# Half-height score products of two head pairs in one visit instead of two, from batch 3 on

## The chip, the cores and the metric

The kernel runs on one core of one Trainium2 chip. The metric is the device time of one execution in microseconds; of several runs the median is given. Before the change it is 300.1 us, the median of three runs (300.06 to 301.02). All durations below come from one profiled execution of that kernel.

## The reference

Two stages in a row. First, attention over 8 batches, 8 heads, 576 positions and 64 channels a head. Heads 0 to 3 see the last 32 positions ("local"), heads 4 to 7 see all earlier positions that are equal modulo 32 ("strided"):

```python
mask_local = (rel >= 0) & (rel < stride)
mask_strided = (rel >= 0) & (pos[None, :] % stride == pos[:, None] % stride)
attn = softmax(where(mask, scale * q @ k.T, -1e9)) @ v      # cut
x = attn_out.transpose(0, 2, 1, 3).reshape(4608, 512)
h = x @ w_in                                  # 512 -> 2048
g = np.maximum(h, 0.0) + alpha * np.minimum(h, 0.0)
return g @ w_out                              # 2048 -> 512
```

Second, the two-layer network on the 4608 tokens that come out. Inputs and output are float32.

## The kernel before

**The network.** The 4608 tokens are taken as nine chunks of 512 (the loop over n from L1019). A chunk has 30 steps. Steps 0 to 15 are *lin1* (`lin1_piece`, L688): one block of 128 hidden units, four products 128x512 (L678) into one of three PSUM banks `hb`, which `hbank` lends in turn; ScalarE makes `neg` (L697), VectorE makes `gT` from `neg` and the bank (L700). Steps 16 to 29 are *lin2* (`lin2_sums`, L775): eight products 128x256 a step (L811), seven block products in place of eight, by a Strassen-like scheme that works on sums of quadrants of `gT` (`gsum`, L760). VectorE makes most of these sums at the start of lin2; three slices of the first one, for k-blocks 0 to 5, are made by GpSimd in lin1 steps 5, 9 and 13. The three `hb` banks serve lin2 as accumulators A, B and C.

**Attention.** Heads go in pairs; pair g is pair g mod 4 of batch g // 4, pairs 0 and 1 of a batch local, 2 and 3 strided. A local pair has six blocks of 96 queries against 128 keys, a strided pair eight blocks of 72 against 72 (positions are sorted by their rest). The two heads of a pair lie in partitions 0 to 63 and 64 to 127, so that a score product uses one half of TensorE's rows, and the products of the two heads alternate: these are the half-height products (L450). `score_both` (L427) computes a pair's scores in two groups: the first into the double bank `sp`, the second into two banks of the three-bank pool `ps` (`sph`). ScalarE takes the exponential into a tile `et` (L464, L474), GpSimd multiplies by the mask (L468, L470, L477). The last exps are kept in the list `defer` and let go one by one by `attn_step` (L653), or at once where a PV piece needs them. `pv_piece` (L486) multiplies masked scores with v (L512, two or three pieces of up to six products a pair, each into a `ps` bank); VectorE divides by the row sum (L521, L523). `x_piece` (L530) transposes the result on TensorE (`xp`, a `ps` bank as well), or a DMA does (`x_dma`).

**The order.** A list of pieces is written out in L577 to L645: the step for g holds the scores of pair g, then the PV pieces of pair g - 1, with transposes, loads and copies between them. In the loop from L1019 a counter takes pieces from this list between the steps of a chunk: about one after each lin2 step, one after every two lin1 steps. `keep` (`keep_in_program_order`) holds every engine to the order in which the program was written, so an instruction that waits holds up what stands behind it on its engine. Scores of local pairs fall into lin2, those of strided pairs into lin1.

Of the kernel before, what the change touches and what calls it, by code (L numbers as in the profile page):

```python
# [9 lines left out]
F32 = mybir.dt.float32  # L10
F16 = mybir.dt.float16
ALU = mybir.AluOpType
AF = mybir.ActivationFunctionType
# [19 lines left out]
def kernel(  # L33
# [42 lines left out]
    mfirst, mother, mstr = mmul[:, 0:288], mmul[:, 96:192], mmul[0:72, 288:360]  # L76
# [22 lines left out]
    kTs = [cpool.tile([128, 2, (768, 672)[i]], F16, name=f"kT{i}") for i in range(2)]  # L99
    vls = [cpool.tile([128, 24, 65], F16, name=f"vl{i}") for i in range(2)]  # L100
    vss = [cpool.tile([128, 4, 8, 65], F16, name=f"vs{i}") for i in range(2)]
    ets = [cpool.tile([128, 800], F16, name=f"et{i}") for i in range(NE)]
    x16s = cpool.tile([80, 1024], F16)
    qks = {nm: cpool.tile([80, 4, 512], F16, name=f"{nm}sd") for nm in "qk"}

# [4 lines left out]
    def load_qk(b, strided, nm):  # L110

        h0 = 4 if strided else 0
        src = q if nm == "q" else k
        if strided and b:
            t16 = hpool.tile([128, 2, 512], F16, tag=f"{nm}s", bufs=2, name=f"{nm}s")
            cast16[(b, True, nm)] = t16
        else:
            t16 = hpool.tile([128, 2, 512], F32, tag=f"{nm}l", bufs=2, name=f"{nm}l")  # L120
            loaded[(b, strided, nm)] = t16
        base = src[b, h0 : h0 + 1, 0:1, :]
        eng = nc.sync if (b > 2 and not strided) or (b == 0 and strided) else nc.gpsimd
        if b == 0 and strided and nm == "q":
            eng = nc.scalar
        keep(eng.dma_start(t16, bass.AP(
            tensor=base.tensor, offset=base.offset,
            ap=[[8 * D, 64], [2 * S * D, 2], [S * D, 2], [1, 8 * D]])))
# [30 lines left out]
            keep(nc.sync.dma_start_transpose(o, qks[nm].rearrange("p h c -> p (h c)")))  # L159

    def cast_s(b, nm, eng):
        t16 = hpool.tile([128, 2, 512], F16, tag=f"{nm}s", bufs=2, name=f"{nm}s")
# [77 lines left out]
    def make_pair(g):  # L240
        P = Pair()
        P.g, P.b, P.hp = g, g // 4, g % 4
        P.strided = P.hp >= 2
        P.pr = P.hp % 2
        P.n, P.w = (8, 72) if P.strided else (6, 96)
        u = g // 2
        P.dx = P.b >= DX and P.strided
        P.lx = P.b >= LX and not P.strided
        P.xd = P.b >= DX and P.hp < (2 if P.b == DX else 3)
        if P.dx or P.lx:  # L250
            P.qT, P.kT = (z[u % 2].rearrange("r e c -> r (e c)") for z in (qTs, kTs))
# [4 lines left out]
        if P.lx:  # L256
            P.sgroups = ([0, 1, 2, 3], [4, 5])
        P.et = {}
        P.x16 = None
        return P  # L260
# [162 lines left out]
    defer, defer_et = [], {}  # L423
    late = []
    second = {"on": False}

    def score_both(P):  # L427

        w, r = P.w, 72 if P.strided else 128
        for i in range(2):  # L430
            et = ets[ectr["i"] % NE]
            ectr["i"] += 1
            if i:
                sps = [pspool.tile([128, 512], F32, tag="ps", name="sph") for _ in range(2)]
            else:
                sp = pbpool.tile([128, 2, 512], F32, tag="sp", name="sp")
                sps = [sp[:, y] for y in range(2)]
            grp = P.sgroups[i]
            n = w * len(grp)
            for x, t in enumerate(grp):  # L440
                if P.dx:
                    q0 = k0 = 80 * (4 * (2 * P.pr + t % 2) + t // 2)
                elif P.lx:
                    j = 3 * (2 * P.pr + t % 2) + t // 2
                    q0, k0 = 96 * j, 128 * j
                else:
                    q0, k0 = w * t, 32 + 72 * t if P.strided else 96 * t
                for y in range(2):
                    hf = slice(64 * y, 64 * y + 64)
                    keep(nc.tensor.matmul(  # L450
                        sps[y][:, w * x : w * x + w], P.kT[hf, k0 : k0 + 128],
                        P.qT[hf, q0 : q0 + w], start=(x == 0), stop=(x == len(grp) - 1),
                        skip_group_check=True))
                    P.et[(2 * (t // 2) + y, t % 2) if P.dx or P.lx else (t, y)] = (et, n * y + w * x)
            ev = et[0:r, 0 : 2 * n]
            if not P.strided and i == 0 and not P.lx:
                mv = ev.rearrange("r (y c) -> r y c", y=2)
                m = mfirst.unsqueeze(1).to_broadcast([r, 2, n])
            else:
                z = 2 * w if P.lx and i == 0 else 0  # L460
                mv = ev[:, z:].rearrange("r (c f) -> r c f", f=w)
                m = (mstr if P.strided else mother).unsqueeze(1).to_broadcast([r, (2 * n - z) // w, w])
            if i == 0:
                keep(nc.scalar.activation(  # L464
                    ev.rearrange("r (y c) -> r y c", y=2), sp[0:r, :, 0:n], AF.Exp, scale=SCALE))
                if P.lx:
                    fv = ev[:, 0 : 2 * w].rearrange("r (c f) -> r c f", f=w)
                    keep(nc.gpsimd.tensor_tensor(  # L468
                        fv, fv, mfirst[:, 0:96].unsqueeze(1).to_broadcast([r, 2, w]), op=ALU.mult))
                keep(nc.gpsimd.tensor_tensor(mv, mv, m, op=ALU.mult))  # L470
                continue

            def ex(y):
                keep(nc.scalar.activation(  # L474
                    ev[:, n * y : n * y + n], sps[y][0:r, 0:n], AF.Exp, scale=SCALE))
                if y:
                    keep(nc.gpsimd.tensor_tensor(mv, mv, m, op=ALU.mult))  # L477

            defer_et["et"] = et
            if second["on"]:  # L480
                ex(0)
                defer.append(lambda: ex(1))
            else:
                defer.extend([lambda: ex(0), lambda: ex(1)])

    def pv_piece(P, a):  # L486
        run_masks(P)
        while defer and any(P.et[z][0] is defer_et["et"] for z in P.et):
            defer.pop(0)()
        if P.x16 is None:  # L490
            if P.xd and P.strided:
                P.x16 = x16s
# [25 lines left out]
        w = P.w  # L518
# [52 lines left out]
    def Pv(g, i):  # L571
        return lambda: pv_piece(pairs[g], i)
# [4 lines left out]
    for g in range(7, npair + 2):  # L577
        c = g // 4
# [3 lines left out]
        okT = 8 <= t < 4 * LX and (t % 4 == 0 or t < 4 * DX and t % 2 == 0)  # L582
        nP = len(pairs[p].pgroups) if okP else 0
        seq = []
        if okA:
            seq.append(("S", lambda a=a: score_both(pairs[a])))
        if okP:
            seq.append(("P", Pv(p, 0)))
# [7 lines left out]
            seq.append(("Tk", T(t // 2, "k")))  # L596
        if nP == 3:
            seq.append(("P", Pv(p, 2)))
        if not seq:
            seq.append(("N", lambda: None))  # L600

# [51 lines left out]
    def attn_step(end):  # L653
        run_masks()
        if pos["i"] < end:
            pieces[pos["i"]][1]()
            pos["i"] += 1
        while late:
            late.pop(0)()
        if defer:  # L660
            defer.pop(0)()


    gTs = {}
# [94 lines left out]
        }[which]  # L759
        keep(eng.tensor_tensor(o[:, k0:k1], x[:, k0:k1], y[:, k0:k1], op=op))  # L760

    lay, held = {}, {}

    def store(n, i, j, osb, mts=(0, 1)):

# [310 lines left out]
```

## Time and profile before

| what | value |
|---|---|
| median of three runs | 300.1 us (300.06 to 301.02) |
| the profiled execution | 300.0 us, its span 298.1 us |
| VectorE, ScalarE, GpSimd busy | 76%, 58%, 57% of the span |
| the chain that ended last | PE 80%, DMA 11%, POOL 4%, issue 2%, DVE 2%, ACT 1% |
| a lin1 product 128x512, a lin2 product 128x256 | 379 ns, 272 to 273 ns from start to modelled end |
| exp of 576 columns, of 768 | 654 ns (128 partitions), 811 ns |
| a mask of 576, of 384 columns on GpSimd | 1.27 us, 0.91 us |
| a sum of 512, 1024, 2048 columns on VectorE | 538, 683, 1213 ns |
| a slice of the first sum on GpSimd | 1.15 us |

How to read it: PE is TensorE, PEld its weight loads, which run beside the products; DVE is VectorE, ACT ScalarE, POOL GpSimd, SP the queue of SyncE. A line "out<-in" names the tiles; L and a number is the line of the kernel. Ends of products are modelled, starts are recorded, so two products are compared from start to start. In brackets a view shows how long an engine was idle before an instruction, and what released it. The chain is followed back from the last instruction, at each step to what released it.

### The profile page before, as it was taken

The numbers are of one execution on the slowest core, as the hardware profiler recorded it, in microseconds if no ns is written. First come the engines' busy times: TensorE is split into PE (matmuls) and PEld (weight loads), VectorE is DVE, ScalarE is ACT, GpSimd is POOL, SyncE is SP. The second block draws the span as 40 slices with busy tenths as digits, with TensorE's granted clock in tenths as the row PEclk, the third lists the DMA queues.
The fourth block names the chain that finished last, engine by engine and source line by source line (L and its number), as shares of the span: only waits on it lengthen the run. The fifth ranks groups of instructions, "written<-read, shape, count | busy, mean of one in ns | idle before, by whom it ended". The sixth has DMA issues, their size and how long they took to land.

```text
span 298.1 us, 7107 instructions
## 1 busy us (share of the span) xinstructions
PE 289.9 (97%) x2808; PEld 193.6 (65%) x2808; DVE 227.8 (76%) x427; ACT 173.5 (58%) x325; POOL 168.5 (57%) x182
## 2 busy tenths in 40 slices
PE   7899998999999999999999999999999999999995
PEld 3664445644886478646898887468746864784584
DVE  5788868979975988488848894889488858946872
ACT  3566556888557773776377636763676257406620
POOL 8952289359757996777777778665555003101300
PEclk9999999999999999999999999999999999999999
DMA  7999999995998969999999999993811140022004
GB/s 219 204 202 207 205 238 266 170 175 178 177 154 186 111 100 127 173 192 160 132 209 177 138 141 182 184 144 54 201 22 21 24 141 0 2 71 73 0 2 141
DMA packets 102273, 41.01 MB, mean 138 GB/s; under 512 B 80720, under 2 KB 99424, under 8 KB 102240
## 3 DMA queue, kind: packets, MB, share of 16 engines
q0 software_dynamic: 56336, 19.25, 61.1%
q1 hardware_dynamic: 45632, 20.78, 35.3%
q10 hardware_dynamic: 272, 0.52, 0.6%
q8 instruction: 22, 0.36, 0.6%
q14 instruction: 11, 0.09, 0.1%
HBM read 38.60 MB, written 9.44 MB: 161 GB/s over the span
## 4 chain that ended last, share of the span: by engine, by line
PE 80%; DMA 11%; POOL 4%; issue 2%; DVE 2%; ACT 1%; POOLq 0%
PE hb L678 36%; PE hb L811 32%; DMA ks<-in_k_dram 6%; PE pv L512 4%; DMA win<-in_moe_w_in_dram 3%; PE sp L450 2%; DMA ql<-in_q_dram 2%; PE hb L715 2%; PE opl L811 1%; PE xp L533 1%; PE tp L280 1%; DVE gT L700 1%; PE sph L450 1%; POOL ql L217 1%; POOL vl L205 0%
## 5 line engine op out<-in xcount | busy, mean ns | idle before, releaser
L678 PE MATMUL hb<-xT,win 128*128 128x512 f16 (+1 forms) x616 | 127.2, 357 | 0.0
L700 DVE SCALAR_TENSOR_TENSOR gT<-neg,oma,hb 128x512 f16<-128x512 f32 x138 | 100.7, 744 | 33.0 <-ACT neg L697 26.3
L697 ACT ACTIVATE neg<-hb 128x512 f32<-128x512 f32 x138 | 82.1, 597 | 32.7 <-PE hb L678 31.5
L678 PEld LDWEIGHTS <-win 128*128 128x128 f16 x640 | 60.0, 98 | 53.8
L760 POOL TENSOR_TENSOR gsum<-gT 128x512 f16<-128x512 f16 x23 | 26.5, 1152 | 68.9 <-DVE gT L700 68.9
L811 PEld LDWEIGHTS <-gsum 128*128 128x128 f16 x512 | 47.3, 98 | 6.0 <-DVE gsum L760 0.5
L811 PEld LDWEIGHTS <-gT 128*128 128x128 f16 x384 | 35.9, 98 | 6.0 <-issue 0.5
L470 POOL TENSOR_TENSOR et<-et,mmul 128x576 f16<-128x576 f16 (+1 forms) x24 | 30.6, 1274 | 14.6 <-issue 7.8
L823 ACT COPY o<-hb 128x512 f32<-128x512 f32 (+1 forms) x32 | 18.1, 569 | 32.5 <-PE hb L811 32.5
L523 DVE TENSOR_TENSOR x<-pv,rc 96x384 f16<-96x384 f32 (+2 forms) x65 | 34.5, 531 | 2.2
L811 PE MATMUL hb<-wout,gT 128*128 128x256 f16 x248 | 30.8, 273 | 0.1
L811 PE MATMUL hb<-wout,gsum 128*128 128x256 f16 x248 | 30.5, 272 | 0.0
L811 PE MATMUL hb<-wsum,gsum 128*128 128x256 f16 x248 | 30.3, 273 | 0.0
L477 POOL TENSOR_TENSOR et<-et,mmul 72x576 f16<-72x576 f16 (+2 forms) x24 | 29.3, 1220 | 0.4 <-ACT et L474 0.4
L826 DVE TENSOR_TENSOR o<-hb,o 128x512 f32<-128x512 f32 (+1 forms) x24 | 16.3, 681 | 17.0 <-PE hb L811 12.5
L464 ACT ACTIVATE et<-sp 72x576 f16<-72x576 f32 (+2 forms) x24 | 16.4, 685 | 20.6 <-PE sph L450 17.2
L512 PEld LDWEIGHTS <-et 72*128 72x128 f16 (+1 forms) x416 | 21.9, 98 | 8.0 <-issue 1.3
L474 ACT ACTIVATE et<-sph 72x288 f16<-72x288 f32 (+2 forms) x48 | 17.8, 388 | 0.0
L521 DVE RECIPROCAL rc<-pv 72x6 f32<-72x6 f32 (+2 forms) x80 | 14.5, 181 | 2.9 <-PE pv L512 2.4
L715 PE MATMUL hb<-wout,gT 128*128 128x512 f16 x64 | 15.6, 379 | 0.2 <-ACT osb L720 0.2
L811 PE MATMUL hb<-wsum,gT 128*128 128x256 f16 x120 | 15.3, 273 | 0.0
L760 DVE TENSOR_TENSOR gsum<-gT 128x512 f16<-128x512 f16 (+2 forms) x17 | 14.7, 865 | 0.2
(117 smaller groups left out, 318.0 us busy)
## 6 DMA issues: line engine op xcount, KB each, us to landing
out_dram<-o SPq DMA_DIRECT2D x31, 256.0 KB, 3.1
stv<-in_v_dram POOLq DMA_DIRECT2D x8, 288.0 KB, 8.4
vl<-in_v_dram POOLq DMA_DIRECT2D x6, 384.0 KB, 9.3
wout<-in_moe_w_out_dram POOLq DMA_DIRECT2D x4, 512.0 KB, 16.9
qsd<-in_q_dram POOLq DMA_DIRECT2D x6, 288.0 KB, 7.6
ksd<-in_k_dram POOLq DMA_DIRECT2D x6, 288.0 KB, 7.1
kl<-in_k_dram SPq DMA_DIRECT2D x3, 512.0 KB, 5.1
ql<-in_q_dram POOLq DMA_DIRECT2D x3, 512.0 KB, 6.4
```

The lines of the kernel that those rows point to most:

```text
L470: keep(nc.gpsimd.tensor_tensor(mv, mv, m, op=ALU.mult))
L474: keep(nc.scalar.activation(ev[:, n * y : n * y + n], sps[y][0:r, 0:n], AF.Exp, scale=SCALE))
L477: keep(nc.gpsimd.tensor_tensor(mv, mv, m, op=ALU.mult))
L512: keep(nc.tensor.matmul(pv[:, 65 * x : 65 * x + 65], et[0:r, c : c + 128], v16[0:r, 2 * P.pr + hh, t, :] if P.strided else v16[:, 6 * (2 * ...
L523: keep(nc.vector.tensor_tensor(P.x16[0:w, c0 : c0 + 64 * nb].rearrange("r (c e) -> r c e", e=64), pvv[:, :, 0:64], rc[0:w, 0:nb].unsqueeze ...
L678: keep(nc.tensor.matmul(hps[:, dst : dst + w], win16[:, kk, 128 * m : 128 * m + 128], xT[:, kk, src : src + w], start=(first and kk == kks ...
L697: keep(nc.scalar.activation(neg, hps, AF.Relu, scale=-1.0))
L700: keep(nc.vector.scalar_tensor_tensor(gTs[n][:, m, :], neg, oma[:, m : m + 1], hps, op0=ALU.mult, op1=ALU.add))
L715: keep(nc.tensor.matmul(ops, gTs[n][:, kf, 128 * mt : 128 * mt + 128], wout16[:, kf, :], start=(kf == 0), stop=(kf == 15)))
L760: keep(eng.tensor_tensor(o[:, k0:k1], x[:, k0:k1], y[:, k0:k1], op=op))
L811: keep(nc.tensor.matmul(dst, lhs[:, kf, 128 * mt : 128 * mt + 128], rhs[:, kf, :], start=(first and own and kf == 0), stop=(kf == 7), skip ...
L823: keep(nc.scalar.copy(o, x))
```

## The change

From batch 3 on (`units`), the scores of both pairs of a unit (two local or two strided pairs of a batch) are computed in one visit, `score_unit`. It stands at the end of the step of the unit's first pair, behind the PV pieces of the pair before, with an empty piece ("N") ahead of it and one behind. The step of the unit's second pair has no scores. Batch 2 keeps `score_both`.

A visit uses six banks: `sp` (two) for all but the last block of the first pair A, three `ps` banks, and one lin1 bank or, in lin2, accumulator C before its use. c3 and c4 take the last block of both pairs, for one head each, c1 and c2 the other blocks of pair B. Exps go into new tiles: e1 for A, e2 for B (two sets of each, 1088 wide), e3 for the last blocks. The order on ScalarE is c4, e1, then c3, c1, c2, of which the last three (in lin2 the last two) go through `defer`, now a list of tiles and functions. Masks are two operations for e1, one for e3, two for e2.

```diff
-    ets = [cpool.tile([128, 800], F16, name=f"et{i}") for i in range(NE)]
+    ets = [cpool.tile([128, 640], F16, name=f"et{i}") for i in range(NE)]
+    evs = [[cpool.tile([128, 1088], F16, name=f"ev{i}{j}") for j in range(2)] for i in range(2)]
...
-            t16 = hpool.tile([128, 2, 512], F16, tag=f"{nm}s", bufs=2, name=f"{nm}s")
+            t16 = evs[b]["qk".index(nm)][:, 0:1024].rearrange("p (f c) -> p f c", f=2)
...
+    def score_unit(u):
+        A, Bp = pairs[2 * u], pairs[2 * u + 1]
+        w, r, nb = A.w, 72 if A.strided else 128, 7 if A.strided else 5
+        n = nb * w
+        (e1, e2), e3 = evs[u % 2], ets[u % 2]
+        sp = pbpool.tile([128, 2, 512], F32, tag="sp", name="sp")
+        c3, c1, c2 = [pspool.tile([128, 512], F32, tag="ps", name="sph") for _ in range(3)]
+        c4 = lay["Cf"] if second["on"] else hbank()
+        rest = [(A, nb), (Bp, nb)]
+        streams = [
+            [(A, s, sp[:, 0], w * s) for s in range(nb)]
+            + [(P, s, c3, w * z) for z, (P, s) in enumerate(rest)]
+            + [(Bp, s, c1, w * s) for s in range(nb)],
+            [(A, s, sp[:, 1], w * s) for s in range(nb)]
+            + [(P, s, c4, w * z) for z, (P, s) in enumerate(rest)]
+            + [(Bp, s, c2, w * s) for s in range(nb)],
+        ]
+        for x in range(2 * nb + 2):
+            for y in range(2):
+                P, s, o, c = streams[y][x]
...
+                hf = slice(64 * y, 64 * y + 64)
+                keep(nc.tensor.matmul(
+                    o[:, c : c + w], P.kT[hf, k0 : k0 + 128], P.qT[hf, q0 : q0 + w],
+                    start=(c == 0), stop=(c == (1 if s == nb else nb - 1) * w), skip_group_check=True))
...
+        def masks(e):
+            ev = e[0:r, 0 : 2 * n]
+            if A.lx:
+                fv = ev[:, 0 : 2 * w].rearrange("r (c f) -> r c f", f=w)
+                mask(fv, mfirst[:, 0:96].unsqueeze(1).to_broadcast([r, 2, w]))
+                fv = ev[:, 2 * w :].rearrange("r (c f) -> r c f", f=w)
+                mask(fv, mother.unsqueeze(1).to_broadcast([r, 2 * nb - 2, w]))
+                return
+            k = 4 if A.strided else 3
...
+        ex(e3[0:r, 2 * w : 4 * w], c4[0:r, 0 : 2 * w])
+        ex(e1[0:r, 0 : 2 * n].rearrange("r (y c) -> r y c", y=2), sp[0:r, :, 0:n])
+        masks(e1)
+        if second["on"]:
+            ex3()
+        else:
+            defer.append(((e3,), ex3))
+        defer.append(((e2,), lambda: ex(e2[0:r, 0:n], c1[0:r, 0:n])))
+        defer.append(((e2,), ex2))
...
-        while defer and any(P.et[z][0] is defer_et["et"] for z in P.et):
-            defer.pop(0)()
+        used = [P.et[t, y][0] for t in P.pgroups[a] for y in range(2)]
+        while any(e is z for es, _ in defer for e in es for z in used):
+            defer.pop(0)[1]()
...
-        if okA:
+        units = g >= 4 * (DX + 1)
+        visit = okA and units and a % 2 == 0
+        if okA and not units:
             seq.append(("S", lambda a=a: score_both(pairs[a])))
...
+        if visit:
+            seq.append(("N", lambda: None))
+            seq.append(("S", lambda a=a: score_unit(a // 2)))
+            seq.append(("N", lambda: None))
...
-            for t in ets:
-                keep(nc.gpsimd.memset(t[:, 640:800], 0.0))
+            for t in evs[0] + evs[1]:
+                keep(nc.gpsimd.memset(t[:, 1024:1088], 0.0))
```

The tiles `evs` also serve, in batches 0 and 1, as the staging tiles of the strided q and k. The branches of `score_both` for the transposed local layout (`P.lx`, batches 5 to 7) go, since those batches are now units.

More of the change, by code (lines that the diff above doesn't have):

```diff
@@ L161, in cast_s @@
     def cast_s(b, nm, eng):
-        t16 = hpool.tile([128, 2, 512], F16, tag=f"{nm}s", bufs=2, name=f"{nm}s")
+        t16 = evs[b]["qk".index(nm)][:, 0:1024].rearrange("p (f c) -> p f c", f=2)
         if eng[0] == eng[1]:
@@ L255, in make_pair @@
         P.pgroups = ([0, 1, 2], [3, 4, 5], [6, 7]) if P.strided else P.sgroups
-        if P.lx:
-            P.sgroups = ([0, 1, 2, 3], [4, 5])
         P.et = {}
@@ L421, in score_piece, with mask, ex, ex3 @@
         keep(nc.gpsimd.tensor_tensor(ev, ev, m, op=ALU.mult))
-    defer, defer_et = [], {}
+    defer = []
     late = []
+    lay = {}
     second = {"on": False}
+    def score_unit(u):
[18 more added lines that the diff above has]
+                P, s, o, c = streams[y][x]
+                if P.dx:
+                    q0 = k0 = 80 * (4 * (2 * P.pr + s % 2) + s // 2)
+                elif P.lx:
+                    j = 3 * (2 * P.pr + s % 2) + s // 2
+                    q0, k0 = 96 * j, 128 * j
+                else:
+                    q0, k0 = w * s, 96 * s
+                hf = slice(64 * y, 64 * y + 64)
+                keep(nc.tensor.matmul(
+                    o[:, c : c + w], P.kT[hf, k0 : k0 + 128], P.qT[hf, q0 : q0 + w],
+                    start=(c == 0), stop=(c == (1 if s == nb else nb - 1) * w), skip_group_check=True))
+                key = (2 * (s // 2) + y, s % 2) if P.dx or P.lx else (s, y)
+                P.et[key] = (e3, 2 * w * y + c) if s == nb else (e1 if P is A else e2, n * y + c)
+        def mask(v, m):
+            keep(nc.gpsimd.tensor_tensor(v, v, m, op=ALU.mult))
+        def masks(e):
[7 more added lines that the diff above has]
+            k = 4 if A.strided else 3
+            fv = ev.rearrange("r (y c) -> r y c", y=2)
+            if A.strided:
+                m = mstr
+                for lo, hi in ((0, k), (k, nb)):
+                    mask(fv[:, :, w * lo : w * hi].rearrange("r y (c f) -> r y c f", f=w),
+                         m.unsqueeze(1).unsqueeze(1).to_broadcast([r, 2, hi - lo, w]))
+            else:
+                mask(fv[:, :, 0 : w * k], mfirst.unsqueeze(1).to_broadcast([r, 2, w * k]))
+                mask(fv[:, :, w * k :].rearrange("r y (c f) -> r y c f", f=w),
+                     mother.unsqueeze(1).unsqueeze(1).to_broadcast([r, 2, nb - k, w]))
+        def ex(o, i):
+            keep(nc.scalar.activation(o, i, AF.Exp, scale=SCALE))
+        def ex3():
+            ev = e3[0:r, 0 : 4 * w]
+            ex(ev[:, 0 : 2 * w], c3[0:r, 0 : 2 * w])
+            mask(ev.rearrange("r (c f) -> r c f", f=w),
+                 (mstr if A.strided else mother).unsqueeze(1).to_broadcast([r, 4, w]))
+        def ex2():
+            ex(e2[0:r, n : 2 * n], c2[0:r, 0:n])
+            masks(e2)
+        ex(e3[0:r, 2 * w : 4 * w], c4[0:r, 0 : 2 * w])
[3 more added lines that the diff above has]
+            ex3()
+        else:
+            defer.append(((e3,), ex3))
+        defer.append(((e2,), lambda: ex(e2[0:r, 0:n], c1[0:r, 0:n])))
+        defer.append(((e2,), ex2))
@@ L442, in score_both @@
                     q0 = k0 = 80 * (4 * (2 * P.pr + t % 2) + t // 2)
-                elif P.lx:
-                    j = 3 * (2 * P.pr + t % 2) + t // 2
-                    q0, k0 = 96 * j, 128 * j
                 else:
@@ L453, in score_both @@
                         skip_group_check=True))
-                    P.et[(2 * (t // 2) + y, t % 2) if P.dx or P.lx else (t, y)] = (et, n * y + w * x)
+                    P.et[(2 * (t // 2) + y, t % 2) if P.dx else (t, y)] = (et, n * y + w * x)
             ev = et[0:r, 0 : 2 * n]
-            if not P.strided and i == 0 and not P.lx:
+            if not P.strided and i == 0:
                 mv = ev.rearrange("r (y c) -> r y c", y=2)
@@ L459, in score_both @@
             else:
-                z = 2 * w if P.lx and i == 0 else 0
-                mv = ev[:, z:].rearrange("r (c f) -> r c f", f=w)
-                m = (mstr if P.strided else mother).unsqueeze(1).to_broadcast([r, (2 * n - z) // w, w])
+                mv = ev.rearrange("r (c f) -> r c f", f=w)
+                m = (mstr if P.strided else mother).unsqueeze(1).to_broadcast([r, 2 * n // w, w])
             if i == 0:
@@ L465, in score_both @@
                     ev.rearrange("r (y c) -> r y c", y=2), sp[0:r, :, 0:n], AF.Exp, scale=SCALE))
[L466 to L469, printed above, removed]
                 keep(nc.gpsimd.tensor_tensor(mv, mv, m, op=ALU.mult))
@@ L477, in ex @@
                     keep(nc.gpsimd.tensor_tensor(mv, mv, m, op=ALU.mult))
-            defer_et["et"] = et
             if second["on"]:
                 ex(0)
-                defer.append(lambda: ex(1))
             else:
-                defer.extend([lambda: ex(0), lambda: ex(1)])
+                defer.append(((et,), lambda: ex(0)))
+            defer.append(((et,), lambda: ex(1)))
     def pv_piece(P, a):
         run_masks(P)
-        while defer and any(P.et[z][0] is defer_et["et"] for z in P.et):
-            defer.pop(0)()
+        used = [P.et[t, y][0] for t in P.pgroups[a] for y in range(2)]
+        while any(e is z for es, _ in defer for e in es for z in used):
+            defer.pop(0)[1]()
         if P.x16 is None:
@@ L660, in attn_step @@
         if defer:
-            defer.pop(0)()
+            defer.pop(0)[1]()
     gTs = {}
@@ L760, in g_sum @@
         keep(eng.tensor_tensor(o[:, k0:k1], x[:, k0:k1], y[:, k0:k1], op=op))
-    lay, held = {}, {}
+    held = {}
     def store(n, i, j, osb, mts=(0, 1)):
```

## The prediction

> **What bounds the kernel now.** I read four views in this order. The page first, for the busy engine and its clock:
>
> ```profile
> PE 289.9 (97%) x2808; PEld 193.6 (65%) x2808; DVE 227.8 (76%) x427; ACT 173.5 (58%) x325; POOL 168.5 (57%) x182
> ...
> PEclk9999999999999999999999999999999999999999
> ```
>
> TensorE is busy for 97% of 298.1 us, at full clock in every slice. Whatever makes it issue later lengthens the run; work elsewhere counts only when TensorE waits for it. Next the timeline of PE alone (start, duration, group), in the lin1 half and in the lin2 half of a chunk:
>
> ```profile
> 125.41 0.35 PE L512 MATMUL pv<-vl,et 128*128 128x65 f16 x6
> 125.59 2.75 PE L678 MATMUL hb<-xT,win 128*128 128x512 f16 x12
> 128.28 0.30 PE L450 MATMUL sp<-qT,kT 64*128 64x72 f16 x8
> 128.41 0.29 PE L450 MATMUL sph<-qT,kT 64*128 64x72 f16 x8
> 128.64 2.76 PE L678 MATMUL hb<-xT,win 128*128 128x512 f16 x12
> ...
> 141.26 1.91 PE L811 MATMUL hb<-wsum,gsum 128*128 128x256 f16 x16
> 143.10 0.34 PE L450 MATMUL sp<-qT,kT 64*128 64x96 f16 x8
> 143.28 0.25 PE L450 MATMUL sph<-qT,kT 64*128 64x96 f16 x4
> 143.47 1.05 PE L811 MATMUL hb<-wsum,gsum 128*128 128x256 f16 x8
> 144.59 0.34 PE L512 MATMUL pv<-vs,et 72*128 72x65 f16 x6
> ```
>
> Ends are modelled, so I count from start to start. Spacings: 0.216 us for a 512-wide L678 product (8 from 131.43 to 133.15), 0.109 for a 256-wide L811 product, 0.034 or 0.045 for a pair of half-height score products (four pairs from 128.28 to 128.41, or 143.10 to 143.28). Twelve L678 products from 125.59 end at 128.18; the scores start at 128.28: 0.10 lost on entering. Eight score pairs take 0.27 of the 0.36 until 128.64: 0.09 lost on leaving. The lin2 half gives the same (141.26 + 16 x 0.109 = 143.00; scores at 143.10). A PV piece costs nothing of the kind (122.82 + 12 x 0.216 = 125.41). So a **visit to half height costs 0.19 us**. Walking through all starts from 59 us on I find no other loss above 0.26 us between products, and no wait on masks at all. One small wait shows above: eight L811 products end at 144.34, PV starts at 144.59.
>
> **Part 1, fewer visits: -1.9.** Batches 3 to 7 have four visits each, twenty in all; afterwards two each, ten. The number of products does not change (32 in a strided unit, 24 in a local one), nor their alternation between halves. 10 x 0.19 = 1.9 us, all of it on TensorE.
>
> **Part 2, a lost wait: -0.7.** The 0.25 us before 144.59 (also once in each of the next two batches) is PV's wait for a `ps` bank that VectorE still reads: two of the three banks had just gone to the scores. With the local visit moved behind these PV pieces, that piece takes a bank read long before. 3 x 0.25 = 0.7.
>
> **Part 3, local visits: a new wait, +5.9.** In before a pair's scores are followed by the PV pieces of the pair before, a whole step of cover. In the changed program's order on PE the local visit is followed by only 16 L811 products (batches 3, 4) or 24 (5 to 7), and then by the first PV piece of its own first pair, whose weight loads wait on GpSimd. How long the masks take, from the timeline of all engines at two local visits and the timeline of POOL:
>
> ```profile
> 114.05 0.30 PE L450 MATMUL sp<-qT,kT 64*128 64x96 f16 x6
> ...
> 114.67 0.68 ACT L464 ACTIVATE et<-sp 128x576 f16<-128x576 f32 x1
> ...
> 115.44 1.27 POOL L470 TENSOR_TENSOR et<-et,mmul 128x576 f16<-128x576 f16 x1 [2.74 <-ACT et L464]
> ...
> 116.68 1.26 POOL L477 TENSOR_TENSOR et<-et,mmul 128x576 f16<-128x576 f16 x1
> ```
>
> ```profile
> 143.55 0.81 ACT L464 ACTIVATE et<-sp 128x768 f16<-128x768 f32 x1 [0.63 <-PE sph L450]
> ...
> 144.37 1.21 DVE L760 TENSOR_TENSOR gsum<-gT 128x2048 f16<-128x2048 f16 x1
> 144.45 1.54 POOL L468 TENSOR_TENSOR et<-et,mmul 128x192 f16<-128x192 f16 x1 [1.94 <-ACT et L464]
> ```
>
> ```profile
> 150.81 0.56 POOL L468 TENSOR_TENSOR et<-et,mmul 128x192 f16<-128x192 f16 x1
> ```
>
> The first score product starts at T. TensorE: 12 pairs x 0.045 + 0.09 = 0.63, then 16 x 0.109 = 1.74: PV is reached at T+2.4; with 24 products at T+3.25.
> Masks: the bank c4, whose exp is first on ScalarE, gets its last product with pair seven, T+0.27; exp starts 0.31 behind the product it needs (143.24 to 143.55): T+0.58. Its 192 columns hold ScalarE 0.21 (two such exps take 0.55 with 0.34 for the last). The exp of e1 has 960 columns: 0.81 for 768 plus 0.16 per 192 (0.81 less 0.65) = 0.97, done at T+1.76. GpSimd starts 0.09 later (144.36 to 144.45): T+1.85. Then 576 columns (1.24 from start to start, 115.44 to 116.68) and 384 (0.90, L477's shape in the groups): T+3.99. In batches 5 to 7 it is 192 (0.51) and 768 (1.27 + 0.36): the same. PV can start 0.1 behind: T+4.1.
> Waits: 2 x (4.1 - 2.4) + 3 x (4.1 - 3.25) = 3.4 + 2.5 = 5.9 us. Behind the waiting weight load stands all of TensorE's queue, in order, so nothing fills the gap. Bounds: the shortest PV could need is the first mask alone, T+3.2, which is 1.6 us in all (its last products read columns of the second, so I do not take it); the longest is one more us in each of batches 4 to 6, where GpSimd first has two loads (1.24, 1.45), two copies (1.03 each) and another load (0.8) in its queue: 8.9.
> Two smaller waits hide in this one: the bank c2, which VectorE may still read, and lin2's bank C, from which c4's exp must read first (batch 4, 0.3).
>
> **Part 4, strided visits: +2.7.** They stand in lin1. The neg of the last piece holds ScalarE until T+0.6 (136.04, 136.15, 136.64 in before); then 0.2 and 1.0 for 1008 columns, GpSimd at T+1.9, 1.24 and 0.99: T+4.1. TensorE reaches PV at 0.67 + 12 x 0.216 + 8 x 0.109 = T+4.1 in batches 4 to 6, later in 3 and 7: no wait. But GpSimd still owes the e3 mask (0.7), the third piece of gsum (1.15) and both e2 masks (2.2), up to T+8.2; before had one mask there. That runs into VectorE's sums at the start of lin2, and these two do not run side by side: above, a 192-wide mask beside a sum took 1.54 instead of 0.56, and the other way round (timeline of all engines):
>
> ```profile
> 108.79 1.28 POOL L477 TENSOR_TENSOR et<-et,mmul 72x576 f16<-72x576 f16 x1
> 109.13 1.24 DVE L760 TENSOR_TENSOR gsum<-gT 128x512 f16<-128x512 f16 x1
> ```
>
> that sum takes 0.42 where nothing is in its way (139.76), and TensorE then lost 0.17 at 110.15. Bounds per batch, 4 to 7: 0.2 from that row; 1.7 if all is done in turn (gsum piece and masks 3.4, sums 0.42 + 2 x 0.64 = 1.7, from T+4.8 to T+9.9, wanted at T+8.2). I take 0.6: the row's 0.17 with three operations instead of one, and 0.1 for the loan of a third lin1 bank to c4. Batch 3 is two pieces further from lin2: 0.3. 4 x 0.6 + 0.3 = 2.7; ends 1 and 7.
>
> The Trainium skill, page "SBUF — State Buffer", section "Who interferes with whom", speaks against the change here: a VectorE operation with two SBUF inputs and a GpSimd operation that reads SBUF exclude each other, and the second waits out the first. Both rows agree; by the rule taken whole this part would stand at its upper end, and the sum at 310.
>
> **Costs at nothing.** The masks' total width is the same; exps go from six to five per unit; ScalarE and GpSimd have 42% to spare. The staging tiles change name only. Four narrow memsets for six (0.25 each, 40.8 us) end earlier in front of a load that waits 2.1 us for ScalarE anyway. The e3 and e2 masks of a local unit have the rest of lin2 and three lin1 pieces as cover; without it they would cost another 3 us per unit.
>
> **Sum.** On the profiled execution (300.0 us around a span of 298.1; median of the three runs 300.1): 300.0 - 1.9 - 0.7 + 5.9 + 2.7 = 306.0, on the median's footing **306.1 us**.
>
> **Rivals.**
> - A, faster: the masks are in time. Then 300.0 - 2.6 and 0.5 for the strided part: 297.9. It hangs on one place, the first PV behind a local visit: it needs masks within 2.4 to 3.25 us of the first score product. For it: TensorE waits on no mask in before. Against: 0.97 of exp and 2.1 of masking alone are 3.1, in sequence. It decides if the five waits together stay below the 2.6 gained. Chance 0.10.
> - B, no change: waits near the lower bounds (1.6 and 1) eat the gain: 300.0. That the visits save nothing, because the switch inside a visit from one bank to the next costs as much, would come to the same with waits of this size. Chance 0.05.
> - C, worse: VectorE and GpSimd take turns at every sum, and GpSimd is late for the local masks too: 300.0 - 2.6 + 8.9 + 4.0 = 310.3. For it: 1.54 and 1.24 above. Against: 0.17 was all that TensorE lost. Chance 0.20.
> - The forecast: 0.65, itself between 302 and 309.
>
> Faster or slower by 0.3% is about what a measurement of this kernel can tell from no change: faster 0.10, within 0.05, slower 0.85. The range leaves out A, B's better half and the far end of C: 301.0 to 310.5.
>
> **What would show it.** In the profile after: ten entries of 0.10 from batch 3 on, not twenty; five waits of PE's weight loads in front of PV on ev tiles, for GpSimd's masks, 0.8 to 1.7 us each; masks beside VectorE sums stretched, or sums of 0.42 stretched past 1; no wait like that before 144.59. I am wrong if PV on ev starts 16 or 24 products behind the local visit without a gap, or if the sums keep their 0.42 and 0.68.

## The result and the profile after

The changed kernel takes **324.3 us**, the median of four runs (322.9 to 325.9), against 300.1 us before (four runs, 299.7 to 301.0): **1.080 times the time before, 95% interval 1.073 to 1.087**. The forecast was 306.1 us with a range to 310.5: the sign was right, the size was not. The profiled execution took 323.0 us around a span of 321.2, that is 23.1 us more than the span before.

The page of the changed kernel first, TensorE's busy time and the clock, and the chain that ended last:

```profile
PE 297.2 (93%) x2808; PEld 194.0 (60%) x2808; DVE 240.4 (75%) x427; ACT 172.9 (54%) x315; POOL 174.3 (54%) x184
...
PEclk9999999999987999999999999999999999999999
...
PE 49%; DVE 13%; DMA 13%; POOL 10%; issue 7%; ACT 6%; POOLq 0%; DVEq 0%; ACTq 0%
```

TensorE's share fell from 97% to 93% with the same 2808 products, two slices lost clock, and of the chain, which was 80% TensorE, only 49% is left. What TensorE waits for, from the waits view (total, times, longest; PEld are weight loads, PE the products behind them, so a wait can stand in both):

```profile
PEld L890 <- DVE gsum L839: 9.6, 19, 1.1
PEld L585 <- POOL ev L463: 7.3, 7, 4.9
...
PEld L890 <- POOL gsum L839: 2.2, 5, 0.7
...
PEld L585 <- DVE x16s L596: 2.0, 1, 2.0
```

Lin2 (L890) waits 24 times for sums, VectorE's or GpSimd's slice, and PV (L585) 7 times for GpSimd's masks; before, the view had no wait for a mask of GpSimd's at all, and 0.5 us in 2 waits for sums.

Where the time went shows best by halves of chunks, from the first lin1 or lin2 product to the first of the next half (us). Halves that are not listed changed by at most 0.1 in the changed kernel. The last three columns are experiments that come below: copies behind (e1), strided visit at the head (e5), local masks on VectorE (e6).

| half | holds | before | after | e1 | e5 | e6 |
|---|---|---|---|---|---|---|
| lin2, chunk 1 | local visit of batch 3 | 16.75 | 23.31 | 18.16 | 24.43 | 16.72 |
| lin1, chunk 2 | strided visit of batch 3 | 15.51 | 16.91 | 16.00 | 16.90 | 16.50 |
| lin2, chunk 2 | its masks, local visit of batch 4 | 15.59 | 19.21 | 17.40 | 16.80 | 18.46 |
| lin2, chunk 3 (4 and 5 within 0.03 of it before and after) | masks of strided, local visit | 14.84 | 17.88 | 17.77 | 15.18 | 17.71 |
| lin2, chunk 6 | masks of strided visit | 13.37 | 15.72 | 15.72 | 13.48 | 15.72 |

So 8.0 us are lost in the two halves around batch 3's local visit (6.56 + 1.40; 0.49 of the 1.40 is still there in e1, where that visit no longer waits long) and 15.1 at the other starts of lin2 (3.6, three times 3.0, 2.4).

**Batch 3's local visit.** The timeline of the changed kernel, ACT, PE and POOL lines; the visit began at 87.80:

```profile
88.63 0.96 ACT L486 ACTIVATE ev<-sp 128x960 f16<-128x960 f32 x1
...
89.45 1.04 PE L890 MATMUL hb<-wsum,gT 128*128 128x256 f16 x8
...
91.06 2.01 POOL L218 COPY vs<-stv 72x1024 f16<-72x1024 f16 x2 [8.34 <-DMA stv<-in_v_dram]
93.02 0.72 POOL L198 DMA_DIRECT2D stv<-in_v_dram  x1
93.76 2.15 POOL L463 TENSOR_TENSOR ev<-ev,mmul 128x576 f16<-128x576 f16 x2
...
95.10 0.40 PE L585 MATMUL pv<-vl,ev 128*128 128x65 f16 x4 [4.61 <-POOL ev L463]
...
95.96 0.29 PE L585 MATMUL pv<-vl,ev 128*128 128x65 f16 x2 [0.46 <-POOL ev L463]
...
96.54 1.90 PE L890 MATMUL hb<-wsum,gT 128*128 128x256 f16 x8
```

The exp of e1 had ended at 89.59 and GpSimd was idle. But ahead of the masks in its queue stand the two `vs` copies, which `cast_v` puts into the first pieces of every fourth step, and these wait for the DMA of `stv`. PV waits 4.61 us for the masks behind them. The last row shows a second loss: eight lin2 products take 1.70 us from start to start (96.54 to 98.24) instead of 0.87. The table of windows shows it. A row has the window and its length, the busy time of PE, PEld, DVE, ACT and POOL (with the number of instructions), the granted clock, the share of the DMA engines and GB/s:

```profile
88.00:90.50 2.50, 2.49 (x40) 1.88 (x32) 0.89 (x2) 2.10 (x5) 0.00 (x0) 1.00 1.35 74
90.50:95.10 4.60, 0.00 (x1) 0.01 (x1) 0.00 (x0) 0.25 (x1) 4.03 (x5) 0.80 0.94 229
95.10:98.20 3.10, 2.64 (x22) 1.99 (x23) 0.74 (x2) 0.64 (x1) 3.10 (x4) 0.50 0.73 94
98.20:100.50 2.30, 2.30 (x9) 0.88 (x7) 0.00 (x0) 0.90 (x2) 2.30 (x3) 0.59 0.22 75
```

From 95.1 to 98.2 the granted clock was 0.50, and it was back at 1.00 only from 100.1 on: another 1.7 us in 13 products.

In the timeline of before, the same copies waited too, with the masks of that step ahead of them:

```profile
85.59 1.27 POOL L470 TENSOR_TENSOR et<-et,mmul 128x576 f16<-128x576 f16 x1 [2.35 <-ACT et L464]
...
86.83 1.26 POOL L477 TENSOR_TENSOR et<-et,mmul 128x576 f16<-128x576 f16 x1
...
91.58 1.04 POOL L217 COPY vs<-stv 72x1024 f16<-72x1024 f16 x1 [3.49 <-DMA stv<-in_v_dram]
```

**Starts of lin2.** The timeline of before at chunk 3, DVE lines; GpSimd's last mask ended at 139.87 there:

```profile
139.76 0.42 DVE L760 TENSOR_TENSOR gsum<-gT 128x512 f16<-128x512 f16 x1
140.10 1.28 DVE L760 TENSOR_TENSOR gsum<-gsum,gT 128x1024 f16<-128x1024 f16 x2
```

The timeline of the changed kernel at the same place, POOL, DVE and PE lines:

```profile
151.35 1.15 POOL L839 TENSOR_TENSOR gsum<-gT 128x512 f16<-128x512 f16 x1
...
151.67 1.12 DVE L839 TENSOR_TENSOR gsum<-gT 128x512 f16<-128x512 f16 x1
...
152.47 2.86 POOL L463 TENSOR_TENSOR ev<-ev,mmul 72x576 f16<-72x576 f16 x2
...
152.71 3.17 DVE L839 TENSOR_TENSOR gsum<-gsum,gT 128x1024 f16<-128x1024 f16 x2
...
154.53 0.61 PE L890 MATMUL hb<-wsum,gsum 128*128 128x256 f16 x4 [0.29 <-DVE gsum L839]
...
155.94 0.61 PE L890 MATMUL hb<-wsum,gsum 128*128 128x256 f16 x4 [0.80 <-DVE gsum L839]
```

The 512-column sum takes 1.12 instead of 0.42, beside GpSimd's slice; the two 1024-column sums take 3.17 instead of 1.28, beside the e2 masks. From start to start TensorE loses 0.24, 0.46, 0.96, 0.33 and 0.49 there (the last two at PV and behind it, with VectorE in arrears), 2.5 us in the chunk.

### The profile page after: what moved, and what is told of

Its sections match the earlier page's. It is cut to its first block, busy times and chain, and to the rows that moved or that the text cites. A ratio compares the mean times of both kernels' runs of the same rounds, so it can differ in the third digit from the quotient of the medians.

```text
span 321.2 us, 7078 instructions
## 1 busy us (share of the span) xinstructions
PE 297.2 (93%) x2808; PEld 194.0 (60%) x2808; DVE 240.4 (75%) x427; ACT 172.9 (54%) x315; POOL 174.3 (54%) x184
## 4 chain that ended last, share of the span: by engine, by line
PE 49%; DVE 13%; DMA 13%; POOL 10%; issue 7%; ACT 6%; POOLq 0%; DVEq 0%; ACTq 0%
PE hb L757 27%; PE hb L890 15%; DVE gsum L839 6%; DMA ev<-in_k_dram 6%; DVE gT L779 3%; DMA win<-in_moe_w_in_dram 3%; ACT neg L776 3%; DMA stv<-in_v_dram 3%; POOL ev L463 3%; DVE x L596 2%; PE pv L585 2%; ACT ev L486 2%; DMA ql<-in_q_dram 2%; PE hb L794 2%; POOL vs L218 1%
## 5 line engine op out<-in xcount | busy, mean ns | idle before, releaser
L757 PEld LDWEIGHTS <-win 128*128 128x128 f16 x640 | 60.9, 98 | 57.1 <-issue 3.8
L463 POOL TENSOR_TENSOR ev<-ev,mmul 72x576 f16<-72x576 f16 (+5 forms) x40 | 46.1, 1162 | 29.4 <-ACT ev L486 28.6
L890 PEld LDWEIGHTS <-gsum 128*128 128x128 f16 x512 | 45.8, 98 | 16.8 <-DVE gsum L839 9.6
L890 PEld LDWEIGHTS <-gT 128*128 128x128 f16 x384 | 36.7, 99 | 6.4 <-issue 0.8
L890 PE MATMUL hb<-wsum,gsum 128*128 128x256 f16 x248 | 33.0, 273 | 5.2 <-DVE gsum L839 4.5
L890 PE MATMUL hb<-wout,gsum 128*128 128x256 f16 x248 | 30.7, 273 | 1.0 <-DVE gsum L839 1.0
L890 PE MATMUL hb<-wout,gT 128*128 128x256 f16 x248 | 30.6, 272 | 0.4 <-ACT et L486 0.3
L585 PEld LDWEIGHTS <-ev 72*128 72x128 f16 (+1 forms) x240 | 14.0, 98 | 14.3 <-POOL ev L463 7.3
L218 POOL COPY vs<-stv 72x1024 f16<-72x1024 f16 x12 | 18.0, 1527 | 8.3 <-DMA stv<-in_v_dram 8.3
L839 DVE TENSOR_TENSOR gsum<-gsum,gT 128x1024 f16<-128x1024 f16 x16 | 19.5, 1257 | 0.0
L839 DVE TENSOR_TENSOR gsum<-gT 128x512 f16<-128x512 f16 (+2 forms) x17 | 18.4, 1081 | 0.2
L890 PE MATMUL hb<-wsum,gT 128*128 128x256 f16 x120 | 16.1, 282 | 0.0
L214 ACT COPY xT<-xp 128x576 f16<-128x576 f16 x11 | 7.0, 639 | 16.8 <-PE xp L606 16.7
```

Source lines behind the costliest of these rows:

```text
L218: keep(nc.gpsimd.tensor_copy(o, i))
L463: keep(nc.gpsimd.tensor_tensor(v, v, m, op=ALU.mult))
L585: keep(nc.tensor.matmul(pv[:, 65 * x : 65 * x + 65], et[0:r, c : c + 128], v16[0:r, 2 * P.pr + hh, t, :] if P.strided else v16[:, 6 * (2 * ...
L757: keep(nc.tensor.matmul(hps[:, dst : dst + w], win16[:, kk, 128 * m : 128 * m + 128], xT[:, kk, src : src + w], start=(first and kk == kks ...
L890: keep(nc.tensor.matmul(dst, lhs[:, kf, 128 * mt : 128 * mt + 128], rhs[:, kf, :], start=(first and own and kf == 0), stop=(kf == 7), skip ...
```

## The experiments

Theories K and L were: K, masks that are wanted at once stand behind copies that wait for a load; L, GpSimd's operations and VectorE's sums do not run side by side. The rivals were in turn a chain of exps that is too long by itself, VectorE late for another reason, and half-height visits that cost something wherever they stand. Where no range is given the time is that of one run; the time before was 299.4 to 300.6 us on those chips.

**e1, copies behind the visit.** `nslots` lists the pieces of a step that can carry a copy; in a step with a visit only the last is left.

```diff
+        if visit:
+            nslots = nslots[-1:]
```

> The changed kernel, with the two vs copies of a batch on GpSimd issued in the last empty piece of the local visit's step, behind the visit, instead of in the step's first pieces. Theory K: in the second half of chunk 1 the e1 masks of batch 3 stood in GpSimd's queue behind copies that wait 8.3 us for the DMA of stv, which cost TensorE 5.5 us before the first PV piece, and then about 1.6 us at half clock. Then the wait falls to the 1.6 of batch 4, lin2 of chunk 1 from 23.3 to about 19 us, lin1 of chunk 2 from 16.9 back to 15.5: about 5.7 us less, 318. Rival: the masks were late for their own sake (exp and masks in sequence); then nothing moves, 324. The lin2 halves of chunks 2 to 6 should stay within 0.5 us of the changed kernel's 19.2, 17.9, 17.9, 17.9, 15.7.

316.3 us. Lin2 of chunk 1 falls from 23.31 to 18.16, and the clock stays at 1.0 throughout. K holds for batch 3. The starts of lin2 in chunks 3 to 6 keep their loss (17.8 to 18.4, and 15.7). That of chunk 2 falls from 19.21 to 17.40, more than expected: its 1024-column sums, 2.96 with the copies next in GpSimd's queue, take 1.28 without them.

**e2 and e3, one kind of visit alone.** The other kind is scored as before the change (from batch 3 on with four `et` tiles).

```diff
-        units = g >= 4 * (DX + 1)
+        units = g >= 4 * (DX + 1) and g % 4 < 2      # e2; e3: g % 4 >= 2
```

> One part alone: only local pairs go in one visit, strided pairs are scored pair by pair at the head of their steps as before the change. Lock theory (GpSimd's e2 masks and its slice of the first sum against VectorE's sums at the start of lin2, about 12 us over five batches, all of it from the strided visits): the lin2 halves of chunks 3 to 5 come out at before's 14.84 plus 0.6, that of chunk 6 at before's 13.4, chunk 1 stays at 23; in all 300.1 + 9 - 1 = 308 to 311. Rival (the sums are late because of what local visits leave behind on the engines): the halves of chunks 3 to 6 stay 2 us or more above before, 318 or more.

> The other part alone: only strided pairs go in one visit, local pairs pair by pair as before the change (score tiles of batches from 3 on turn over four buffers instead of six). Lock theory: the starts of lin2 keep their loss of 2 to 2.5 us in each of chunks 2 to 6, chunk 1 is as before (16.8), no half clock at the start of chunk 2: 300.1 + 12 - 1 = 309 to 312, and the sums of 1024 columns beside masks stay at 1.5 to 1.76 us. Rival: 302 or less.

e2 313.5 us, above the range and below the rival's 318: lin2 of chunks 3 to 5 falls to 15.29, of chunk 6 to 13.38, as before; batch 3 keeps its wait and its half clock. e3 318.5 us, more than expected: the loss at the starts stays from chunk 3 on, and lin2 of chunk 3 rises to 21.05. In it a local score visit waits 1.75 for VectorE, a sum of 2048 columns then takes 4.79 beside masks and copies, and the granted clock is 0.50 from 147.4 to 154.2 (and once more from 184.9 to 188.3). This run does not price the strided visits cleanly, but chunk 1 is as before (16.76) and the late sums are there. So the local visits do the damage in batch 3, and the strided ones most of that at the starts of lin2.

**e4, the strided e2 masks on VectorE.** `mask` takes an engine; for e2 of a strided unit it is `nc.vector`.

> The changed kernel with the two e2 masks of strided visits on VectorE instead of GpSimd; nothing else moved. Lock theory: VectorE then runs its masks and its sums one after the other, the 1024-column sums go back to 0.68 us, and only the slice of the first sum still collides (1.1 instead of 0.42): lin2 of chunks 3 to 5 from 17.9 to about 16.3, of chunk 6 from 15.7 to 14.3, in all 6 to 8 us less, 317. Rival (backlog): lin2 starts late because five exps on ScalarE hold up neg, and with it gT and the sums that need it; then VectorE, which gets 1 us of masks more per visit, makes it later still: 325 or more, with the sums at 0.68 all the same.

325.1 us, a miss for L as I had put it. VectorE masks e2 ahead of the last gT (150.44, 2.42 for both, beside GpSimd's e3 mask and slice), gT is done at 153.52 instead of 151.64, and the sums begin so much later. The 1024-column sums still take 1.52 each, now with the `vs` copies next in GpSimd's queue. The move changed the order on VectorE too, so that it could not tell what the masks on GpSimd cost.

**e5, the strided visit at the head of its step.**

```diff
+            if g % 4 == 0:
+                seq += [gap, vis, gap]
+            else:
+                seq = [vis] + seq + [gap, gap]
```

> The changed kernel with one move: the strided visit stands at the head of its step (some 20 lin1 products, 4.6 us, earlier) and the local visit stays. If the loss at the starts of lin2 is the meeting of GpSimd's masks with VectorE's sums, the masks end before the sums begin, the 512-column sum is back near 0.42 and the 1024-column sums near 0.68, the lin2 halves of chunks 3 to 6 come down from 17.9 to 15.0 to 15.7 (15.7 to 13.4 to 14 in chunk 6), and the span falls by 10 to 13 us, to 308 to 314 us. If the masks only happen to stand there, and VectorE is late for another reason (more work, PV banks that come free late), the sums stay at 1.5 or start late, and the time stays over 320. Batch 3's local visit still loses its 6.5 us in both.

314.4 us, 0.4 above the range. The timeline of this kernel, POOL and DVE, at chunk 3:

```profile
148.57 1.17 POOL L842 TENSOR_TENSOR gsum<-gT 128x512 f16<-128x512 f16 x1
...
150.73 0.42 DVE L842 TENSOR_TENSOR gsum<-gT 128x512 f16<-128x512 f16 x1
...
151.07 1.29 DVE L842 TENSOR_TENSOR gsum<-gsum,gT 128x1024 f16<-128x1024 f16 x2
...
152.32 1.06 POOL L218 COPY vs<-stv 72x1024 f16<-72x1024 f16 x1
```

The masks end at 146.0, the slice before the sums begin, and the sums are back at 0.42 and 2 x 0.64. L holds, against VectorE being late by itself. A new cost appears: lin1 halves of 16.03 instead of 15.4. In chunk 3 lin1 waits 0.32 for a bank at the visit's exit and 0.55 in two places later; the changed kernel had 0.3 of thin waits there.

**e6, the local e1 masks on VectorE.** As e4, for e1 of local units.

> The changed kernel with the e1 masks of the local visits on VectorE; all else stays. If batch 3's visit loses its time because its masks stand behind the two vs copies in GpSimd's queue, which wait for a load, the 4.6-us idle stretch before PV goes or shrinks to under 2 us, and lin2 of chunk 1 falls from 23.3 to 17 to 20; batch 4's chain (T+4.1) gets about 1 us shorter. The starts of lin2 in chunks 3 to 6 keep their 2.4 to 3 us. In sum 317 to 321 us. If the chain itself (exps and bank waits) and not the queue sets PV's start, lin2 of chunk 1 stays over 22 and the time within 1 us of 324.

314.8 us, better than expected. The timeline of this kernel, DVE, PE and POOL:

```profile
89.61 0.73 DVE L463 TENSOR_TENSOR ev<-ev,mmul 128x576 f16<-128x576 f16 x2 [1.43 <-ACT ev L487]
...
90.31 0.35 PE L586 MATMUL pv<-vl,ev 128*128 128x65 f16 x6
...
91.23 1.03 POOL L218 COPY vs<-stv 72x1024 f16<-72x1024 f16 x1 [8.54 <-DMA stv<-in_v_dram]
```

The copies wait as long as ever, PV no longer does: lin2 of chunk 1 is at 16.72, the time before. VectorE needs 0.73 for both masks where GpSimd needs 2.15, so the chain itself (the rival) is shorter as well.

**e7, three moves together:** e1, the strided visit as in e5, and the local visit ahead of the last PV piece.

> Three moves together: the vs copies behind the visit (as in the run of that move alone), the strided visit at the head of its step, the local visit one PV piece earlier with an empty piece behind it. If the two causes (copies that wait ahead of the masks; masks beside the sums) are all of the loss, what stays is the saving of 1.9 + 0.7 us against a residue of local waits of up to 1 us a batch: 298 to 304 us. If the half-height visits carry a loss of their own that no place cures, at least 308.

306.2 us, above the range and below the 308 of the rival. The starts of lin2 are healed, but the local visit in its new place waits inside itself for banks that x on VectorE still reads (0.79 and 0.65 from start to start in batch 5), so lin2 of chunks 3 to 5 stands at 15.88.

**e8, the strided e2 masks left out, and e11, the same with the copies behind the visit.**

> The changed kernel without the second pair's masks (e2) in the strided visits, so that part of the strided scores stays unmasked; nothing takes their place on any engine. This prices the meeting of masks and sums: the lin2 halves of chunks 3 to 5 fall from 17.9 to 15.2 to 16, that of chunk 6 from 15.7 to 13.4 to 14, with the sums back at 0.68 and 0.42 where nothing of GpSimd's stands beside them; 311 to 315 us. If VectorE is late by itself, the sums stay near 1.5 or start as late as before, and the time over 320. The vs copies come up to the sums' time then: if they lock VectorE too, one 1024-column sum of the two stays at 1.5, and the time is 315 to 319.

> The kernel without the strided e2 masks (part of the strided scores stays unmasked) and with the vs copies behind the visit: GpSimd then has only its slice of the sums and the loads beside VectorE's sums. The run without the masks alone kept lin2 at 17.7 us, with both 1024-column sums at 1.52 beside the loads and ahead of the copies. If the copies took the masks' place there, the sums are now at 0.68, lin2 of chunks 3 to 5 is 15.2 to 16.0 and the time 305 to 309. If the issuing of the loads itself slows the sums, they stay at 1.5, lin2 over 17, and the time is 313 to 317.

e8 319.3 us, between its ranges (up to 319) and the rival's (over 320), with lin2 of chunks 3 to 5 still at 17.6 to 17.7; e11 307.4 us, with 15.9, as expected. The timelines of e8 and then e11 at chunk 3, POOL and DVE:

```profile
149.74 1.15 POOL L840 TENSOR_TENSOR gsum<-gT 128x512 f16<-128x512 f16 x1
...
150.01 1.17 DVE L840 TENSOR_TENSOR gsum<-gT 128x512 f16<-128x512 f16 x1
...
150.83 1.25 POOL L143 DMA_DIRECT2D qx<-in_q_dram  x1
...
151.09 2.96 DVE L840 TENSOR_TENSOR gsum<-gsum,gT 128x1024 f16<-128x1024 f16 x2
...
152.07 1.44 POOL L143 DMA_DIRECT2D kx<-in_k_dram  x1
...
153.51 1.44 POOL L218 COPY vs<-stv 72x1024 f16<-72x1024 f16 x1
```

```profile
143.07 1.14 POOL L842 TENSOR_TENSOR gsum<-gT 128x512 f16<-128x512 f16 x1
...
143.33 1.17 DVE L842 TENSOR_TENSOR gsum<-gT 128x512 f16<-128x512 f16 x1
...
144.17 1.24 POOL L143 DMA_DIRECT2D qx<-in_q_dram  x1
...
144.43 1.28 DVE L842 TENSOR_TENSOR gsum<-gsum,gT 128x1024 f16<-128x1024 f16 x2
...
145.40 1.44 POOL L143 DMA_DIRECT2D kx<-in_k_dram  x1
```

Up to kx both engines do the same at the same distances. Only where the copies follow do the two sums take 2.96 instead of 1.28. So without the masks it is the copies that slow the sums here, and the issuing of loads costs the sums nothing. In chunk 6 of e8 no copies follow: the sums take 1.28, and the half is 14.23. How the copies do it stays open. Their recorded start lies behind the first slowed sum (spans on GpSimd are recorded roughly), and in e5, above, they follow just as closely at 152.32 while the sums ahead of them take 1.29.

**e9 and e10, e5 and e6 together,** e10 with the strided visit behind the first PV piece of its step instead of at its head.

> The strided visit at the head of its step and the local e1 masks on VectorE, the two moves that each took some 10 us off alone (314.4 and 314.8 of 324.3). If the two causes are separate places that do not touch each other, the sum is 324.3 - 9.9 - 9.5 = 304.9: 303.5 to 306.5. What stays above 300 would then be waits of the half-height visits themselves: about 1 us a batch (lin1 halves 16.0 instead of 15.4, lin2 halves 15.2 instead of 14.8). If the moves share a cause (one wait that both shorten), the sum is less than the parts, and the time is 308 to 314.

> As the run with both moves, but the strided visit stands behind the first PV piece of its step, 1.5 to 4 us later. If the 0.6 us that the lin1 halves lose with the visit at the head is its wait for a bank beside the x of the last PV piece, it goes, the masks still end just ahead of the sums, and the time is 301 to 304. If the masks then reach the sums (a 512-column sum at 1.1, 1024-column sums over 0.7), the lin2 halves go back up by 0.7 to 2 us each and the time is 306 to 314.

e9 306.6 us (305.9 to 307.0), ratio 1.020 (1.017 to 1.023), 0.1 us over its range: the moves save nearly the sum of their parts, 17.7 of 19.4. What stays is lin1 at 16.03, and batch 3, where e3's mask is now the one behind the copies. This kernel's timeline, POOL and PE:

```profile
92.83 2.01 POOL L218 COPY vs<-stv 72x1024 f16<-72x1024 f16 x2 [10.59 <-DMA stv<-in_v_dram]
...
96.51 0.23 PE L586 MATMUL pv<-vl,et 128*128 128x65 f16 x2 [2.46 <-POOL et L463]
```

e10 312.2 us (311.5 to 315.5), ratio 1.042 (1.036 to 1.048). It went the second way, though not by the masks, which end as the slice begins (146.6): the slice meets the 512-column sum (1.34), loads and copies follow, and the 1024-column sums take 1.52 as in e8. The profiled execution is the slowest of the four, 315.5 us; 2.7 of it were lost in chunk 0, ahead of all visits.

**e12 and e13, local visits alone, with their e1 masks on VectorE;** e12 in all batches, e13 from batch 5 on.

> Half-height visits in the local steps alone (the strided score pieces as before the change) and the local e1 masks on VectorE. The local visits alone gave 313.5, of which 6.5 and 1 to 2 us were batch 3's wait and the half clock behind it. If that was GpSimd's queue, the time is now 301 to 305, with lin2 of chunk 1 at 16.7 to 17 and those of chunks 3 to 5 at 14.8 to 15.3. Whether it comes under 300 shows if a half-height visit pays at all: five of them save at most 5 x 0.19 us and the bank waits. If VectorE's masks push its sums or gT back, lin2 of chunks 3 to 5 is over 15.5 and the time over 306.

> Half-height visits only in the local steps of batches 5 to 7 (three of the ten), with the first pair's local masks on VectorE; batches 3 and 4 and all strided steps as before the change. With the local visits in all batches a pair of halves from chunk 3 on was 0.2 us shorter than before (lin2 14.44 instead of 14.84, lin1 15.52 instead of 15.33), and the whole 1.6 us longer for batches 3 and 4. If the saving is real, three batches give 3 x 0.2 us: 299.2 to 299.8 against 300.1, lin2 of chunks 3 to 5 at 14.4 to 14.5. If the two quarters cancel (what lin2 gains, lin1 loses), 300.0 to 300.4. If the move to VectorE costs something elsewhere, over 300.5.

| half | before | e12 | e13 |
|---|---|---|---|
| lin1, chunk 2 | 15.51 | 16.82 | 15.51 |
| lin2, chunk 2 | 15.59 | 16.22 | 16.80 |
| lin1, chunks 3, 4, 5 | 15.33, 15.47, 15.33 | 15.52, 15.66, 15.51 | 15.51, 15.66, 15.51 |
| lin2, chunks 3, 4, 5 | 14.84, 14.84, 14.83 | 14.44 each | 14.44 each |

e12 301.7 us, ratio 1.004 (1.002 to 1.006); in batch 3 PV still waits 0.85 for e3's mask, which stands behind the copies. e13 **299.6 us against 300.3, ratio 0.997 (0.995 to 0.999)**: the one version here that is faster than both kernels. Each of the three batches gains 0.21 us (0.40 less in lin2, 0.19 more in lin1, where six PV products stand now), as expected. In e13's profiled execution chunk 2, scored in the old way, loses 1.21: the slice and a mask fell beside the 1024-column sums (its timeline, DVE and POOL):

```profile
94.06 2.02 POOL L218 COPY vs<-stv 72x1024 f16<-72x1024 f16 x2 [4.97 <-DMA stv<-in_v_dram]
...
110.19 1.37 POOL L850 TENSOR_TENSOR gsum<-gT 128x512 f16<-128x512 f16 x1
...
110.48 3.32 DVE L850 TENSOR_TENSOR gsum<-gsum,gT 128x1024 f16<-128x1024 f16 x2
...
111.53 1.72 POOL L561 TENSOR_TENSOR et<-et,mmul 72x576 f16<-72x576 f16 x1
```

The copies had waited for their load until 94.06, against 91.58 in before, and GpSimd's queue stayed some 2.5 us later up to these masks (lin2 began only 1.0 later): the copies' wait again, in a step that e13 leaves as it was. Most executions of e13 can hardly have this loss. The profiled one took 301.5 us, the slowest of twelve; its span of 299.7 is the 298.1 of before, 1.0 more ahead of the first lin1 product, 1.2 here and 0.6 less in the three batches. Nine of the other spans are 297.4 to 297.9, against a median of 298.5 before: 0.6 to 1.1 less, with no room for 1.2 more. They left no profile, so this is argued, not shown.

## Why the prediction was right in sign and wrong in size

- **Part 1 (-1.9), right.** Ten visits are entered with 0.10 each. That a visit less is worth 0.19 shows in a whole time only in e13, at 0.21 a batch.
- **Part 2 (-0.7), right and of little use.** The 0.25 ahead of that PV piece went in all three chunks. In e13 a wait of 0.22 ahead of a later lin2 product stands in its place.
- **Part 3 (+5.9), right in its chain, wrong in batch 3.** In batch 4 the chain came out as worked out. The timeline of the changed kernel, ACT, POOL and PE, with T = 128.19:

```profile
129.02 0.96 ACT L486 ACTIVATE ev<-sp 128x960 f16<-128x960 f32 x1
...
130.07 2.14 POOL L463 TENSOR_TENSOR ev<-ev,mmul 128x576 f16<-128x576 f16 x2 [5.16 <-ACT ev L486]
...
131.40 0.30 PE L585 MATMUL pv<-vl,ev 128*128 128x65 f16 x4 [0.31 <-POOL ev L463]
...
132.27 0.24 PE L585 MATMUL pv<-vl,ev 128*128 128x65 f16 x2 [0.58 <-POOL ev L463]
```

  The masks began at T+1.88 (forecast 1.85) and the last PV products at T+4.08 (4.1); lost at PV 1.2 us (1.7), since four products needed only the first mask, and 0.36 for c4's exp (0.3, which I took to be hidden). Batches 5 to 7 lost 0.64 each (0.85), 0.50 of it already inside the visit, for a bank. The step that failed is "2 x (4.1 - 2.4)" for batch 3: 5.5 us in two waits (4.77 and 0.68 from start to start) instead of 1.7, and 1.7 more at half clock. Part 3 measured 10.7 in all. I had the copies in my upper bound, but "in each of batches 4 to 6" and at the 1.03 us that one lasts, not at what it waits for; the row at 91.58 of before, idle for 3.49 us, was there to read.
- **Part 4 (+2.7), the right mechanism, mis-sized by more than four times.** "The row's 0.17 with three operations instead of one" made 0.6 a batch; measured are 2.5 in batches 4 to 6, 2.2 in 7, and 2.4 in 3 instead of 0.3: 12.1 us. My row was one 512-column sum beside one mask, which it met for 0.94 of the mask's 1.28 us: the sum took 0.82 longer, and TensorE lost only 0.17 of that, because the rest was slack. In the changed kernel the sums of chunk 3 took 0.70 and 1.89 longer, and slack of that kind counts once. The upper end of 1.7 was too low as well: it had each operation once in turn, but behind the late sums stood the x of PV on VectorE (0.33 and 0.49 more), and in batch 3 slice and copies, not masks, met the sums, so that PV waited 1.91 for x16s. Rule and rows pointed the same way; the error was to price a meeting of three operations by what TensorE lost, behind its slack, in a meeting with one.
- **Costs at nothing.** Exps between the negs of lin1 were in this list (ScalarE with 42% to spare). In the lin1 halves of chunks 2 to 6 waits of 0.05 to 0.28 between products come to 1.8 us; before there were none. That the exps cause them was not tested by itself. With the parts above (-1.9 - 0.7 + 10.7 + 12.1) this makes 22.0 of the 23.1 us; the rest, in slower exits and thin gaps, I have not traced.
- **Rivals.** A needed masks within 2.4 to 3.25 us, and they took 4. B needed waits near 1.6 and 1 us, and they were several times that. C named both mechanisms and stopped at 310 for the same two prices.

## What to carry to other kernels

When work moves within an engine's queue, read what stands ahead of it there and what that waits for, not how long it lasts: two copies of 1 us cost 5 us because their load was late. Price a meeting of two engines by the whole overlap and by what is queued behind the slower one; what the critical engine lost in a shorter meeting, part of it hidden by slack, is a lower bound. A saving of 0.2 us a visit survives only where the visit's results are not wanted within the length of its own chain.

## What the runs showed of the hardware

- VectorE's sums of 512 columns took 1.12 to 1.34 instead of 0.42 beside GpSimd's slice, those of 1024 columns 1.76 and 1.49 instead of 0.68 beside masks. Beside the issuing of loads alone they took 0.68.
- Two masks, 960 columns together on 128 partitions, took 0.73 us on VectorE and 2.14 on GpSimd. In contact with GpSimd's e3 mask and slice two masks on 72 partitions (e4) took VectorE 2.42.
- In a gap of 4.6 us in TensorE's products the granted clock fell to 0.50, and lin1 products behind it stood 0.427 apart instead of 0.216; a gap of 2.5 us (e9) left the clock at 1.0. The Trainium skill, page "TensorE: Matmul & The Clock Gate", section "Part 1: The HAM clock gate", has the clock fall to half after an idle window of about 3.4 us; these two gaps agree with it. Two other runs do not. In e3 the clock was 0.50 from 147.4 on, though TensorE had been busy for 1.60 of the 3.41 us ahead and no gap there was longer than 1.6; in e10 it was 0.50 from 51.3 on, behind a gap of 2.4. So the length of one gap does not settle it here, and what does is not shown. By the same section the clock returns after as long a busy window; in the changed kernel the half rate lasted from 95.1 to 99.9.
